# Two more early chunks flipped by TensorE, their masks and products on other engines, and a rebuilt order, in a gated attention with a feed-forward layer

## The chip, the cores and the metric

The kernel runs on one core of a Trainium2 chip. The metric is device microseconds of one execution. Before the change the median of three runs was 541.18 us (540.56 to 541.62).

## The reference

Two layers, in float32. The attention keeps, for each of 4 batches and 8 heads, a 48x48 state that decays by `alpha` at every one of 768 time steps; the feed-forward layer takes its output as 3072 rows of 384.

```python
for t in range(S):                                   # S = 768, q k v alpha: (4, 8, 768, 48)
    state = alpha[:, :, t, :, None] * state + np.einsum('bhd,bhe->bhde', k[:, :, t], v[:, :, t])
    y[:, :, t] = np.einsum('bhd,bhde->bhe', q[:, :, t], state)
x = y.transpose(0, 2, 1, 3).reshape(3072, 384)
h = x @ w_in                                         # (384, 2048), float64 in memory
g = np.where(h >= 1, h, np.where(h <= -1, 0.0, (h + 1) ** 2 / 4))
out = g @ w_out                                      # (2048, 384), float64 in memory
```

## The kernel before

**Chunks.** The sequence is cut into 24 chunks (0 to 23) of 128 time steps, six to a batch. For a chunk, `alpha`, `k` and `q` are wanted with the head dimension on partitions. Chunks below `EARLY` (7) are loaded as they lie, in rows of 48 numbers (192 bytes), and TensorE turns them into PSUM with three *flips* of four transposes each (L521). Later chunks are loaded twice over, by four transfers for each tensor in rows of 768 bytes, and VectorE turns them in SBUF (L534). VectorE then makes two running products of `alpha` (the scans L610 and L636), multiplies the backward one by `k` (L654), and the forward one is multiplied by `q` (L660): by VectorE out of PSUM for chunks 3 to 6 (`HELP` to `EARLY`); by GpSimd out of SBUF for the later ones and for chunks 0 to 2, whose flipped `q` ScalarE copies to SBUF first (L658). TensorE turns the product with `k`: this is the *keys' turn* of the chunk, K0 to K23 (L681). Score products follow (L696), state updates (L709), masks (L781 on VectorE; for half of them, in chunks below `HELP`, ScalarE copies and GpSimd multiplies by a mask, L754 and L760) and the chunk's output products (L835).

**Feed-forward.** Chunks go in groups of three. For each group and each f of 16 (128 columns of `w_in`), TensorE makes a *first product* of nine matmuls (L931); VectorE clips and takes a maximum (L975, L986), ScalarE squares and rounds (L960, L990), GpSimd makes the low part (L991); then come the nine matmuls of the *second product* (L1009). Groups 0 and 1 share each half of the weights: f 0 to 7 for both, then f 8 to 15 for both, then whole groups. First products are numbered here H1 to H128 and second ones F1 to F128, in TensorE's order. The weights come in eight units u0 to u7 of two f, as float64, and each half of a unit (`w_in`, `w_out`) is decoded into two float32 parts by ScalarE, VectorE (L370, L381) and GpSimd (L393, L405, each of which may go to VectorE instead). H7 and H8 are the first that need u3.

**Order.** Nothing is scheduled on the chip: each engine runs its instructions in the order in which the kernel wrote them. The class `Plan` sets that order: it walks through a list of operations with assumed durations and due times (`key`), and at each step takes the one that could start first, or, among those within `NEAR`, the one that is due first. An operation with a second engine is offered to both, there with its due time put off by `LATER`. Buffers count too: of the eight PSUM banks the attention may hold three (six for chunks below `ROOM`, by `FIRST`). Where TensorE would rest more than 0.45 us by the plan, before `WARMTH` of the plan's time, matmuls of zeros (L1080) are put in.

Due times follow from `FETCH` (weights), `DECODE`, `LOAD` (a chunk's loads), `MARGIN` and `AHEAD` (a chunk's own due time, L1088 to L1092).

Of the kernel before, what the change touches and what calls it, by code (L numbers as in the profile page):

```python
# [25 lines left out]
SLACK = 2.0**-15  # L26
GROUP = 3
SHARE = 2
EARLY = 7
MORE = 2  # L30
WARM = 20
LAG = 3.0
FETCH = 12.0
LOAD = 8.0
DECODE = 4.0
PREPARE = 2.5
MARGIN = 9.0
AHEAD = 12.0
FIRST = 6
ROOM = 4  # L40
LATER = 8.0
MERGE = 6
WARMTH = 60.0
HELP = 3
VHELP = 6
SPLIT = 0
CLIPS = 6.0
NEAR = 0.25


class Buf:
# [20 lines left out]
class Plan:  # L72
# [55 lines left out]
            ready.setdefault(way[0], []).append((o, i))  # L128

    def order(self):  # L130
        free = dict.fromkeys(("PE", "DVE", "ACT", "POOL", "SP"), 1.0)
        slots = {name: [(0.0, -i, None) for i in range(n)] for name, (n, share, _) in self.sizes.items() if share == name}
        live = {name: 0 for name in self.sizes}
        left = {}
# [92 lines left out]
def gated_attention_ffn(ctx: ExitStack, tc: tile.TileContext, q, k, v, alpha, w_in, w_out, out):  # L227
# [74 lines left out]
    with ExitStack() as main:  # L302
# [116 lines left out]
        def weights(u):  # L419
            fs = slice(u * NW * P, (u + 1) * NW * P)  # L420
            make = lambda shape, dt: Buf("wt", lambda: wts.tile(shape, dt, name="wt"))
            ti = make([P, KT, NW * P], w_in.dtype)
            to = make([P, NW, DM], w_out.dtype)
            key = need[u]
            pairs_of = w_in[0 : 2 * D * KT, fs].rearrange("(k r e) f -> r e k f", r=2, e=D)
            rest = w_in[2 * D * KT : DM, fs].rearrange("(r k e) f -> r e k f", r=2, k=KT)
            size = P * NW * DM * (8 if wide else 4)
            fetch = key - FETCH
            for r in range(2):
                p = 64 * r  # L430
                plan.op(
                    "SP",
                    Plan.ISSUE,
                    fetch,
                    lambda p=p, r=r: nc.sync.dma_start(out=ti()[p : p + D], in_=pairs_of[r]),
                    [],
                    [ti],
                    moved=size * 3 // 8,
                    beside=r > 0,
                )  # L440
                plan.op(
                    "SP",
                    Plan.ISSUE,
                    fetch,
                    lambda p=p, r=r: nc.sync.dma_start(out=ti()[p + D : p + 64], in_=rest[r]),
                    [],
                    [ti],
                    moved=size // 8,
                    beside=True,
                )  # L450
            plan.op(
                "SP",
                Plan.ISSUE,
                fetch,
                lambda: nc.sync.dma_start(out=to(), in_=w_out[fs, :].rearrange("(j p) m -> p j m", p=P)),
                [],
                [to],
                moved=size,
            )
            wi[u] = make([P, 2, KT, NW, P], F32R)  # L460
            wo[u] = make([P, 2, NW, DM], F32R)
            decode(u, "i", ti, wi[u], "p k f -> p (k f)", key - DECODE)
            decode(u, "o", to, wo[u], "p j m -> p (j m)", key - DECODE + LAG)


        C = CH // 32
# [10 lines left out]
        def load(x, j, key):  # L477
            b, t0 = j // PER, j % PER * CH
            t, rows = raws[x], {"a": alpha, "k": k, "q": q}[x][b, :, t0 : t0 + CH, :]
            if j < EARLY:  # L480
                if j < 2:
                    plan.op("POOL", 0.15, -99, lambda: nc.gpsimd.memset(whole(t, j)[:, :, D:], 1.0), [], [(x, j % 2)])
                plan.op(
                    "SP",
                    Plan.ISSUE,
                    key,
                    lambda: nc.sync.dma_start(out=whole(t, j)[:, :, 0:D], in_=rows.rearrange("h s d -> s h d")),
                    [],
                    [(x, j % 2)],
                    moved=P * DM * 4,  # L490
                )
                return
            if j == EARLY:
                plan.op(
                    "POOL", 0.15, key, lambda: nc.gpsimd.memset(t[:, :, W : W + 32], 1.0), [], [(x, 0), (x, 1)]
                )
            view = rows.rearrange("(g r) (a c) d -> r a g (c d)", r=2, c=C)
            for r in range(2):
                for half in range(2):
                    p0, o = 64 * r + 32 * half, 32 * (1 - half)  # L500
                    plan.op(
                        "SP",
                        Plan.ISSUE,
                        key,
                        lambda p0=p0, o=o, r=r: nc.sync.dma_start(out=t[p0 : p0 + 32, :, o : o + W], in_=view[r]),
                        [],
                        [(x, 0), (x, 1)],
                        moved=P * DM * 2,
                        beside=r + half > 0,
                    )  # L510

        def turned(x, j, key, to=()):

            t = raws[x]
            if j < EARLY:
# [8 lines left out]
                            identity=ident,  # L524
                        )

                flips[j] = plan.op("PE", 0.45, key, flip, [(x, j % 2)], [ps, *to], mode="full", after=[flips[j]] if j in flips else [])
                return ps, view
            o = buf("tp", "turn", [P, G * CH], 2)
            plan.op(  # L530
# [14 lines left out]
        def prepare(j, key):  # L545
# [107 lines left out]
            kt, kT = turned("k", j, key + 0.2)  # L653
            vec(0.66, lambda: nc.vector.tensor_tensor(out=flat(inv()), in0=flat(inv()), in1=kT(), op=ALU.mult), [inv, kt], [inv])  # L654
            qt, qT = turned("q", j, key + 0.2)
            if j < HELP:
                qs = buf("tp", "turn", [P, G * CH], 2)
                plan.op("ACT", 0.55, key + 0.2, lambda qT=qT: nc.scalar.copy(out=qs(), in_=qT()), [qt], [qs])  # L658
                qt, qT = qs, lambda: qs()
            mul = lambda e: e.tensor_tensor(out=flat(Q()), in0=flat(Q()), in1=qT(), op=ALU.mult)  # L660
            in_ps = HELP <= j < EARLY
            ways = [("DVE", 0.66, lambda: mul(nc.vector), not in_ps), ("POOL", 1.3, lambda: mul(nc.gpsimd), True)]
            (e, us, emit, port), other = ways if in_ps else reversed(ways)
            plan.op(e, us, key + 0.3, emit, [Q, qt, last], [Q], port=port, other=None if in_ps else other)
# [76 lines left out]
        def follow(j, key):  # L741
# [5 lines left out]
            for r, to in enumerate((Q, other)):  # L747
                for u in range(2):
                    if r and j < HELP:
# [7 lines left out]
                            beside=True,  # L757
                        )
                        if u:
                            cut = lambda e: e.tensor_tensor(  # L760
                                out=other()[0:HC].rearrange("p g (u t) -> p g u t", u=2),
                                in0=other()[0:HC].rearrange("p g (u t) -> p g u t", u=2),
                                in1=mask[0:HC, None, None, 0:HC].broadcast_to([HC, G, 2, HC]),
                                op=ALU.mult,
                            )
                            plan.op(
                                "POOL",
                                1.35,
                                key,
                                lambda: cut(nc.gpsimd),  # L770
                                [other],
                                [other],
                                port=True,
                                other=("DVE", 0.66, lambda: cut(nc.vector), True),
                            )
                        continue
                    plan.op(
# [309 lines left out]
        for j in range(NCH):  # L1087
            n = max(n for n in range(NG) if first[n] <= j)  # L1088
            since = begin[n - 1] if n > 0 else begin[n] - AHEAD
            due = since + (begin[n] - since) * (j - first[n] + 1) / groups[n] - MARGIN  # L1090
            prepare(j, due - PREPARE)
            attend(j, due)  # L1092
            done = j if j < MERGE or j == NCH - 1 else j - 1
# [173 lines left out]
```

## Time and profile before

| what | value |
|---|---|
| median of three runs | 541.18 us |
| the profiled execution: its time, its span | 542.22 us, 540.4 us |
| busy share of the span: TensorE, VectorE, ScalarE, GpSimd | 95%, 74%, 49%, 51% |
| matmuls of zeros (L1080) in the span | 149, 20.9 us |
| first and second products (L931, L1009) | 1152 matmuls each, 226.1 and 226.2 us |
| mean granted TensorE clock | 0.983 |

The time of an execution is 1.8 us more than its span, which runs from the first to the last instruction. TensorE's busy time counts overlapping matmuls only once, and a waiting TensorE that is given zeros is busy too; so the stretches and the gaps in the order of time say more than the share. "Idle before" is the time in which an engine stood still just ahead of an instruction, with the instruction that released it. DMA shares can pass 1 where transfers cross the edge of a stretch.

### The profile page before, as it was taken

The numbers are of one execution on the slowest core, as the hardware profiler recorded it, in microseconds if no ns is written. First come the engines' busy times: TensorE is split into PE (matmuls) and PEld (weight loads), VectorE is DVE, ScalarE is ACT, GpSimd is POOL, SyncE is SP. The second block draws the span as 40 slices with busy tenths as digits, with TensorE's granted clock in tenths as the row PEclk, the third lists the DMA queues.
The fourth block names the chain that finished last, engine by engine and source line by source line (L and its number), as shares of the span: only waits on it lengthen the run. The fifth ranks groups of instructions, "written<-read, shape, count | busy, mean of one in ns | idle before, by whom it ended". The sixth has DMA issues, their size and how long they took to land.

```text
span 540.4 us, 12713 instructions
## 1 busy us (share of the span) xinstructions
PE 516.0 (95%) x4923; PEld 494.9 (92%) x4923; DVE 399.3 (74%) x709; ACT 265.5 (49%) x490; POOL 276.0 (51%) x295
## 2 busy tenths in 40 slices
PE   8898979998589999999999999999999999999995
PEld 6787869987589999999999999999999999999995
DVE  4789889899988987967968887777787884334332
ACT  4668877676343444344354453444444544333332
POOL 7555888799955525425524543443543543233330
PEclk9989998999989999999999999999999999999999
DMA  9989699934044663334333444335324300101001
GB/s 178 196 173 225 146 210 197 268 74 118 7 111 134 146 154 90 87 79 122 86 77 96 102 105 106 100 61 140 96 45 116 90 16 3 22 1 44 2 0 49
DMA packets 109457, 55.05 MB, mean 102 GB/s; under 512 B 71536, under 2 KB 104272, under 8 KB 109392
## 3 DMA queue, kind: packets, MB, share of 16 engines
q1 hardware_dynamic: 109392, 54.19, 43.2%
q8 instruction: 40, 0.66, 0.5%
q14 instruction: 25, 0.20, 0.1%
HBM read 46.20 MB, written 5.90 MB: 96 GB/s over the span
## 4 chain that ended last, share of the span: by engine, by line
PE 79%; DVE 12%; issue 3%; ACT 2%; POOL 2%; DMA 1%; SPq 0%; DVEq 0%; ACTq 0%; POOLq 0%
PE ps L1009 33%; PE ps L931 33%; PE ps L835 5%; PE ps L709 2%; PE ps L681 2%; DVE w L381 2%; PE ps L1080 2%; PE ps L696 2%; DVE Q L610 2%; DVE inv L636 1%; DVE w L370 1%; DVE meet L649 1%; POOL wt L405 1%; DVE inv L654 1%; DVE gf L986 1%
## 5 line engine op out<-in xcount | busy, mean ns | idle before, releaser
L991 POOL TENSOR_TENSOR gh<-gf,gh 128x384 fp32r<-128x384 f32 x127 | 146.7, 1160 | 162.4 <-ACT gh L990 133.3
L1009 PE MATMUL ps<-wt,gh 128*128 128x384 f32 x1152 | 226.2, 341 | 2.1 <-POOL gh L991 2.1
L931 PE MATMUL ps<-ring,wt 128*128 128x384 f32 x1152 | 226.1, 343 | 1.9 <-POOL wt L405 1.8
L931 PEld LDWEIGHTS ps<-ring,wt 128*128 128x128 f32 x1152 | 205.3, 190 | 3.6 <-POOL wt L405 2.5
L1009 PEld LDWEIGHTS ps<-wt,gh 128*128 128x128 f32 x1152 | 202.9, 189 | 4.3 <-POOL gh L991 3.7
L960 ACT ACTIVATE gf<-gf,half_b 128x384 f32<-128x384 f32 x122 | 75.0, 616 | 114.3 <-DVE gf L975 90.9
L975 DVE TENSOR_SCALAR gf<-ps 128x384 f32<-128x384 f32 x122 | 67.0, 551 | 58.8 <-PE ps L931 50.1
L990 ACT CAST gh<-gf 128x384 fp32r<-128x384 f32 x128 | 65.7, 513 | 74.5 <-DVE gf L986 60.5
L986 DVE TENSOR_TENSOR gf<-gf,ps 128x384 f32<-128x384 f32 x128 | 70.0, 549 | 33.8 <-ACT gf L960 33.3
L728 ACT COPY both<-state 48x192 f32<-48x192 f32 x65 | 22.7, 350 | 45.4 <-POOL state L812 39.8
L405 POOL TENSOR_TENSOR wt<-w,wt 128x768 fp32r<-128x768 f32 x16 | 33.8, 2114 | 4.3 <-ACT wt L404 4.2
L393 POOL TENSOR_TENSOR w<-w,wt 128x768 int32<-128x768 int32 x14 | 27.4, 1960 | 10.1 <-DVE w L381 5.6
L660 POOL TENSOR_TENSOR Q<-Q,turn 128x512 f32<-128x512 f32 x20 | 25.8, 1292 | 7.2 <-DVE turn L534 5.9
L835 PE MATMUL ps<-other,both 128*64 128x64 f32 x372 | 27.9, 225 | 1.6 <-issue 1.5
L812 POOL TENSOR_TENSOR state<-state,last 128x192 f32<-128x192 f32 x20 | 11.3, 567 | 33.5 <-DVE state L738 33.4
L835 PE MATMUL ps<-Q,both 128*64 128x64 f32 x372 | 28.0, 226 | 0.1
L610 DVE TENSOR_TENSOR_SCAN Q<-turn,fwd 128x512 f32<-128x512 f32 x17 | 23.2, 1362 | 6.5 <-PE ps L835 6.4
L835 PEld LDWEIGHTS ps<-Q,both 128*64 128x64 f32 x372 | 24.0, 137 | 3.6 <-issue 1.5
L681 PE MATMUL ps<-ident,inv 128*128 128x128 f32 x96 | 15.2, 282 | 10.8 <-DVE inv L654 10.4
L781 DVE TENSOR_TENSOR Q<-ps,mask 64x256 f32<-64x256 f32 x48 | 20.3, 423 | 6.8 <-ACT other L746 5.3
L835 PEld LDWEIGHTS ps<-other,both 128*64 128x64 f32 x372 | 23.9, 137 | 1.1 <-issue 0.8
L681 PEld LDWEIGHTS ps<-ident,inv 128*128 128x128 f32 x96 | 11.7, 144 | 13.1 <-DVE inv L654 11.1
(89 smaller groups left out, 525.9 us busy)
## 6 DMA issues: line engine op xcount, KB each, us to landing
raw_a<-in_alpha SPq DMA_DIRECT2D x68, 96.0 KB, 2.4
raw_k<-in_k SPq DMA_DIRECT2D x68, 96.0 KB, 2.6
raw_q<-in_q SPq DMA_DIRECT2D x68, 96.0 KB, 2.3
wt<-in_moe_w_out SPq DMA_DIRECT2D x8, 768.0 KB, 9.8
vt<-in_v SPq DMA_DIRECT2D x24, 192.0 KB, 3.1
wt<-in_moe_w_in SPq DMA_DIRECT2D x16, 288.0 KB, 7.3
out<-ot SPq DMA_DIRECT2D x24, 192.0 KB, 2.4
both<-in_v SPq DMA_DIRECT2D x72, 48.0 KB, 2.4
```

The costliest lines, as they stand in the source:

```text
L393: add = lambda e: e.tensor_tensor(out=bits(), in0=bits(), in1=word(I32, 0), op=ALU.add)
L405: sub = lambda e: e.tensor_tensor(out=part(1), in0=data(), in1=part(0).bitcast(F32), op=ALU.subtract)
L610: lambda: nc.vector.tensor_tensor_scan(flat(Q()), aT(), flat(fwd), 0.0, ALU.mult, ALU.max),
L681: nc.tensor.transpose(out=kp()[:, g], in_=K()[:, g], identity=ident)
L835: nc.tensor.matmul(out=ps()[halves[r], to, halves[u]], lhsT=lhsT[:, u, r], rhs=x()[:, g, halves[u]], start=m + u == 0, stop=True, skip_gro ...
L931: nc.tensor.matmul(out=h(), lhsT=win(f, w)[:, kt], rhs=ring[:, at, kt, a, :], start=(m == 0), stop=(m == 3 * KT - 1),)
L960: lambda: nc.scalar.activation(out=gf(), in_=in_(), func=func, scale=scale, bias=bias),
L975: lambda: nc.vector.tensor_scalar(out=gf(), in0=h(), scalar1=-1.0, scalar2=1.0, op0=ALU.max, op1=ALU.min),
L986: lambda: nc.vector.tensor_tensor(out=gf(), in0=gf(), in1=h(), op=ALU.max),
L990: plan.op("ACT", 0.08 + 0.41 * w, key + 0.4, lambda: nc.scalar.copy(out=gh()[:, 0], in_=gf()), [gf], [gh])
L991: sub = lambda e: e.tensor_tensor(out=gh()[:, 1], in0=gf(), in1=gh()[:, 0].bitcast(F32), op=ALU.subtract)
L1009: nc.tensor.matmul(out=o_ps[seg][t](), lhsT=gh()[:, a, (t - c0) * CH : (t - c0 + 1) * CH], rhs=wout(f, w), start=(f == f0 and i == 0), sto ...
```

## The change

Chunks 7 and 8 now count as early ones (`EARLY` 9): their six flips (24 transposes) are TensorE's, into PSUM. No chunk copies its flipped `q` any more (`QHELP` 0), so in chunks 0 to 8 VectorE multiplies by `q` out of PSUM. Chunk 3 joins those whose second masks go over ScalarE and GpSimd (`HELP` 4), and GpSimd cuts with `affine_select` in place of a product with a mask. The other edits are numbers and rules of the plan: due times of loads, decodes and chunks (the first groups get their own margins, unit u0 its own fetch and decode times), `NEAR` 0, `LATER` 4, PSUM banks (`FIRST` 5, `ROOM` 2), zeros allowed up to 165 of the plan's time, and the pads of the early loads as operations of their own.

```diff
-EARLY = 7
+EARLY = 9
-LOAD = 8.0
-DECODE = 4.0
+LOAD = 6.0
+DECODE = 3.0
-MARGIN = 9.0
-AHEAD = 12.0
-FIRST = 6
-ROOM = 4
-LATER = 8.0
+MARGIN = 11.0
+MARGIN0 = 9.0
+MARGIN1 = 6.0
+FETCH0 = 18.0
+DECODE0 = 4.0
+AHEAD = 20.0
+FIRST = 5
+ROOM = 2
+LATER = 4.0
-WARMTH = 60.0
-HELP = 3
+WARMTH = 165.0
+QHELP = 0
+HELP = 4
-NEAR = 0.25
+NEAR = 0.0
...
-            fetch = key - FETCH
+            fetch = key - (FETCH if u else FETCH0)
+            ready = key - (DECODE if u else DECODE0)
...
-            if j < HELP:
+            if j < QHELP:
                 qs = buf("tp", "turn", [P, G * CH], 2)
...
-            in_ps = HELP <= j < EARLY
+            in_ps = QHELP <= j < EARLY
...
                             plan.op(
                                 "POOL",
-                                1.35,
+                                0.62,
                                 key,
-                                lambda: cut(nc.gpsimd),
+                                lambda: nc.gpsimd.affine_select(
+                                    out=other()[0:HC].rearrange("p g (u t) -> p g u t", u=2),
+                                    in_=other()[0:HC].rearrange("p g (u t) -> p g u t", u=2),
+                                    compare_op=ALU.is_ge,
+                                    fill=0.0,
+                                    base=0,
+                                    pattern=[[0, G], [0, 2], [1, HC]],
+                                    channel_multiplier=-1,
+                                ),
...
-            due = since + (begin[n] - since) * (j - first[n] + 1) / groups[n] - MARGIN
+            due = since + (begin[n] - since) * (j - first[n] + 1) / groups[n] - (MARGIN, MARGIN0, MARGIN1)[n + 1 if n < 2 else 0]
```

By the order, matmuls of zeros fall from 149 to 100, four of them behind K6; two subtractions of the decode (L405) move from GpSimd to VectorE and one of its additions (L393) moves back. Three places show how instructions move.

VectorE around the decode of unit u3, the half from `w_in` (before it is `wt_902` into `w_1146`, after `wt_886` into `w_994`; `inv_1167` and `inv_1133` are chunk 6, `inv_949` is chunk 5). Before:

```order
L636 SCALAR_TENSOR_TENSOR inv_1167<-ps_1124,bwd_79 128x511
L986 TENSOR_TENSOR gf_1119<-gf_1119,ps_1072 128x384
L370 TENSOR_SCALAR w_1146<-w_1146 128x768
L381 SCALAR_TENSOR_TENSOR w_1146<-wt_902,w_1146 128x768
L370 TENSOR_SCALAR w_1174<-w_1174 128x768
L649 TENSOR_TENSOR meet_82<-fwd_77,inv_1167 128x4
L986 TENSOR_TENSOR gf_1209<-gf_1209,ps_1133 128x384
L654 TENSOR_TENSOR inv_1167<-inv_1167,ps_1179 128x512
```

After:

```order
L660 TENSOR_TENSOR inv_949<-inv_949,ps_980 128x512
L666 TENSOR_TENSOR Q_924<-Q_924,ps_988 128x512
L386 SCALAR_TENSOR_TENSOR w_883<-wt_531,w_883 128x768
L375 TENSOR_SCALAR w_994<-w_994 128x768
L386 SCALAR_TENSOR_TENSOR w_994<-wt_886,w_994 128x768
L398 ISA w_994<-wt_886,w_994 128x1536
L788 TENSOR_TENSOR Q_924<-ps_1024,mask_65 64x4x64 x2
L788 TENSOR_TENSOR other_1056<-ps_1027,mask_65 64x4x64 x2
L744 TENSOR_TENSOR state_72<-state_72,ps_1024 128x192
L607 TENSOR_SCALAR fwd_77<-ps_1081 128x4
```

The decode stood between chunk 6's second scan and its product with `k`; it now stands ahead of the whole preparation of chunk 6, and its addition is VectorE's own (the row `ISA`). On TensorE, K6 has H6 and F4 ahead of it in both orders.

TensorE around the keys' turn of chunk 8, K8, the row with `inv`. Before:

```order
L1009 MATMUL ps<-wt,gh 128x384 x9
L931 MATMUL ps<-ring,wt 128x384 x9
L1009 MATMUL ps<-wt,gh 128x384 x9
L931 MATMUL ps<-ring,wt 128x384 x18
L681 MATMUL ps<-ident,inv 128x128 x4
L1009 MATMUL ps<-wt,gh 128x384 x9
L709 MATMUL ps<-vt,ks 64x48 x16
```

After:

```order
L527 MATMUL ps<-ident,raw_a 128x128 x4
L527 MATMUL ps<-ident,raw_k 128x128 x4
L1016 MATMUL ps<-wt,gh 128x384 x9
L938 MATMUL ps<-ring,wt 128x384 x9
L527 MATMUL ps<-ident,raw_q 128x128 x4
L1016 MATMUL ps<-wt,gh 128x384 x9
L938 MATMUL ps<-ring,wt 128x384 x9
L687 MATMUL ps<-ident,inv 128x128 x4
L1016 MATMUL ps<-wt,gh 128x384 x9
L938 MATMUL ps<-ring,wt 128x384 x9
```

K8 stood behind H24 and F20, now it stands behind H21 and F18, and the three flips of chunk 8 are in TensorE's own queue just ahead of it. K9 stood behind H28 and F26, now behind H27 and F24.

SP, which issues the loads, behind the loads of chunks 0 and 1 and the second `vt`. Before:

```order
L487 DMA raw_q<-in_q 128x8x48
L556 DMA vt<-in_v 128x8x48
L435 DMA wt<-in_moe_w_in 48x3x256
L445 DMA wt<-in_moe_w_in 16x3x256
```

After:

```order
L562 DMA vt<-in_v 128x8x48
L441 DMA wt<-in_moe_w_in 48x3x256
L451 DMA wt<-in_moe_w_in 16x3x256
L441 DMA wt<-in_moe_w_in 48x3x256
L451 DMA wt<-in_moe_w_in 16x3x256
L461 DMA wt<-in_moe_w_out 128x2x384
L493 DMA raw_a<-in_alpha 128x8x48
L493 DMA raw_k<-in_k 128x8x48
```

Unit u0 of the weights was issued behind the loads of chunks 2 and 3; it now goes ahead of both.

## Rows read from the trace of the kernel before

**Rows 1.** Three stretches, columns: stretch, its length, busy us per engine, clock, DMA.

```profile
0.00:76.00 76.00, 68.68 (x956) 58.69 (x956) 60.88 (x115) 51.65 (x97) 51.13 (x81) 0.98 0.90 188
76.00:170.50 94.50, 83.01 (x665) 79.60 (x666) 83.80 (x121) 55.84 (x95) 75.44 (x52) 0.93 0.56 133
170.50:527.00 356.50, 356.49 (x3263) 349.54 (x3262) 251.95 (x469) 154.30 (x292) 148.37 (x162) 1.00 0.32 77
```

**Rows 2.** TensorE in order of time: start, us, instruction, count, idle before.

```profile
75.99 0.66 PE L681 MATMUL ps<-ident,inv 128*128 128x128 f32 x4 [1.16 <-DVE inv L654]
...
77.21 0.62 PE L931 MATMUL ps<-ring,wt 128*128 128x384 f32 x2
79.62 5.49 PE L931 MATMUL ps<-ring,wt 128*128 128x384 f32 x16 [1.79 <-POOL wt L405]
85.04 0.88 PE L709 MATMUL ps<-vt,ks 64*64 64x48 f32 x32
...
150.06 1.12 PE L681 MATMUL ps<-ident,inv 128*128 128x128 f32 x4 [6.95 <-DVE inv L654]
...
153.92 0.68 PE L709 MATMUL ps<-vt,ks 64*64 64x48 f32 x32
...
167.27 3.34 PE L1009 MATMUL ps<-wt,gh 128*128 128x384 f32 x18
170.45 0.60 PE L681 MATMUL ps<-ident,inv 128*128 128x128 f32 x4
```

**Rows 3.** TensorE's waits from 76 to 170.5: total us, times, longest.

```profile
PE ps L1009 <- POOL gh L991: 1.9, 3, 1.2
```

**Rows 4.** VectorE by line, 76 to 170.5: busy us, mean ns, idle before.

```profile
L975 DVE TENSOR_SCALAR gf<-ps 128x384 f32<-128x384 f32 x21 | 11.4, 547 | 3.1 <-PE ps L931 3.1
L370 DVE TENSOR_SCALAR w<-w 128x768 int32<-128x768 int32 x9 | 8.1, 898 | 1.6 <-ACT w L354 1.6
L610 DVE TENSOR_TENSOR_SCAN Q<-turn,fwd 128x512 f32<-128x512 f32 x3 | 5.9, 1967 | 0.0
L636 DVE TENSOR_TENSOR_SCAN inv<-turn,bwd 128x511 f32<-128x511 f32 x3 | 5.4, 1797 | 0.0
L654 DVE TENSOR_TENSOR inv<-inv,turn 128x512 f32<-128x512 f32 x3 | 3.6, 1199 | 0.1
L534 DVE STREAM_TRANSPOSE turn<-raw_a 128x512 f32<-128x512 f32 x3 | 3.4, 1129 | 0.0
...
L393 DVE CUSTOM_DVE_ANT_0 w<-wt,w 128x1536 uint16<-128x1536 uint16 x1 | 1.8, 1778 | 0.0
```

**Rows 5.** VectorE by line, 0 to 76: the same lines reading PSUM.

```profile
L636 DVE TENSOR_TENSOR_SCAN inv<-ps,bwd 128x511 f32<-128x511 f32 x7 | 8.9, 1271 | 0.0
L610 DVE TENSOR_TENSOR_SCAN Q<-ps,fwd 128x512 f32<-128x512 f32 x7 | 8.6, 1224 | 0.2
...
L654 DVE TENSOR_TENSOR inv<-inv,ps 128x512 f32<-128x512 f32 x7 | 4.8, 686 | 0.6
...
L660 DVE TENSOR_TENSOR Q<-Q,ps 128x512 f32<-128x512 f32 x4 | 2.7, 677 | 0.0
```

**Rows 6.** TensorE from 18 to 32: flips of two chunks, matmuls of zeros.

```profile
19.37 0.66 PE L521 MATMUL ps<-ident,raw_a 128*128 128x128 f32 x4
...
20.74 1.36 PE L1080 MATMUL ps<-zeros 128*128 128x256 bf16 x11
...
27.66 1.11 PE L521 MATMUL ps<-ident,raw_k 128*128 128x128 f32 x4
...
29.42 2.42 PE L1080 MATMUL ps<-zeros 128*128 128x256 bf16 x14
```

**Rows 7.** GpSimd by line, whole span: the masks that it multiplies.

```profile
L760 POOL TENSOR_TENSOR other<-other,mask 64x512 f32<-64x512 f32 x3 | 3.8, 1264 | 0.9 <-ACT other L754 0.8
```

**Rows 8.** Two stretches of ten us, columns as in rows 1.

```profile
10.00:20.00 10.00, 9.11 (x220) 7.67 (x219) 6.59 (x16) 6.30 (x15) 5.80 (x12) 1.00 0.99 193
100.00:110.00 10.00, 10.00 (x61) 9.96 (x59) 9.67 (x14) 5.89 (x10) 6.40 (x7) 1.00 1.06 270
```

More of the change, by code (lines that the diff above doesn't have):

```diff
@@ L130, in order @@
     def order(self):
-        free = dict.fromkeys(("PE", "DVE", "ACT", "POOL", "SP"), 1.0)
+        free = {"PE": 1.0, "DVE": 1.0, "ACT": 1.0, "POOL": 5.0, "SP": 1.0}
         slots = {name: [(0.0, -i, None) for i in range(n)] for name, (n, share, _) in self.sizes.items() if share == name}
@@ L461, in weights @@
             wo[u] = make([P, 2, NW, DM], F32R)
-            decode(u, "i", ti, wi[u], "p k f -> p (k f)", key - DECODE)
-            decode(u, "o", to, wo[u], "p j m -> p (j m)", key - DECODE + LAG)
+            decode(u, "i", ti, wi[u], "p k f -> p (k f)", ready)
+            decode(u, "o", to, wo[u], "p j m -> p (j m)", ready + LAG)
         C = CH // 32
@@ L481, in load @@
                 if j < 2:
-                    plan.op("POOL", 0.15, -99, lambda: nc.gpsimd.memset(whole(t, j)[:, :, D:], 1.0), [], [(x, j % 2)])
+                    plan.op("POOL", 0.15, -99, lambda: nc.gpsimd.memset(whole(t, j)[:, :, D:], 1.0), [], [("pad", x, j)])
                 plan.op(
@@ L525, in flip @@
                         )
-                flips[j] = plan.op("PE", 0.45, key, flip, [(x, j % 2)], [ps, *to], mode="full", after=[flips[j]] if j in flips else [])
+                flips[j] = plan.op("PE", 0.45, key, flip, [(x, j % 2), ("pad", x, j % 2)], [ps, *to], mode="full", after=[flips[j]] if j in flips else [])
                 return ps, view
@@ L759, in follow @@
                         if u:
[L760 to L765, printed above, removed]
                             plan.op(
                                 "POOL",
-                                1.35,
+                                0.62,
                                 key,
-                                lambda: cut(nc.gpsimd),
+                                lambda: nc.gpsimd.affine_select(
[7 more added lines that the diff above has]
+                                ),
                                 [other],
@@ L773, in follow @@
                                 port=True,
-                                other=("DVE", 0.66, lambda: cut(nc.vector), True),
                             )
```

## The prediction, made before the changed kernel ran

> **What bounds the kernel now.** I read the page's strip of 40 slices first, then busy time by stretch, TensorE in order of time, its waits, and VectorE by line. From 170.5 us on TensorE never stops: 356.49 of 356.50 us busy at full clock [rows 1]. Whatever is lost there later would be new; what is lost now is lost before. So the question is how far TensorE's queue has come at some late point of the start. I take the keys' turns K6 (75.99 us) and K9 (170.45 us) as marks [rows 2].
>
> Between the two, by the order, lie H7 to H28 and F5 to F26: 44 products. Two of them, unhindered, take 3.18 us (167.27 to 170.45), so one takes 1.59 and all take 70.0. The stretch is 94.46 long. Its losses: H7 and H8 run from 77.21 to 85.04, 7.83 in place of 3.18, since H7 waits 1.79 us for the subtraction that ends the decode of u3 and the next 16 matmuls run 5.42 us, 0.34 each where 0.18 is usual: 4.65 lost. At K8 TensorE waits 6.95 for VectorE's product with `k`, and K8 with F21 then takes 3.86 where 1.59 and 0.60 are usual: 1.7 more [rows 2]. For GpSimd's low parts the second products wait 1.9 [rows 3]. That makes 15.2; 94.46 less 70.0 and 15.2 leaves 9.3 for the chunks' own matmuls. The granted clock is 0.93 there against 1.00 later [rows 1]; the two slow pieces are on its half level, 1.2 GHz, each behind a wait.
>
> VectorE is behind both big losses: it is busy 83.8 of the 94.5 us, and in the same stretch GpSimd 75.4 [rows 1]. Its operations on two SBUF tiles are long there: the scan L610 takes 1.97 and L654 1.20 [rows 4], against 1.22 and 0.69 where one operand comes out of PSUM [rows 5].
>
> **The change part by part.** *Up to K6.* VectorE makes three more products by `q` there (0.677 each, [rows 5]), and by the order one shift, one maximum, two masks and one ring row fewer, about as much. H6 and F4 stand ahead of K6 as before. VectorE was busy 60.9 of these 76 us [rows 1], so I leave K6 at 76, with -2 and +5 as bounds: unit u0 now loads ahead of chunk 2.
>
> *TensorE from K6 to K9.* It now holds H7 to H27 and F5 to F24: 41 products, 65.2 us. Added are six flips; three flips took from 19.37 to 20.74, so one takes 0.46 and six 2.7 [rows 6]. Four matmuls of zeros at 0.12 (eleven filled 1.36, [rows 6]) make 0.5. With the 9.3 of the chunks the work is 77.7. Then three products are owed before the old K9's state of work: 4.8. Together 82.5 against 94.46: if TensorE never waited, 12.0 us would be won.
>
> *VectorE from K6 to K9.* By the order: six transposes fewer, at 1.11 on the mean of the three tensors (first row [rows 4]): -6.7. Two pairs of scans go from SBUF to PSUM: 2 x (1.967 - 1.224 + 1.797 - 1.271) = -2.5. Two products with `k`: 2 x (1.199 - 0.686) = -1.0. One addition of the decode leaves: -1.8. Two products with `q` come: +1.35. Two subtractions of the decode come to VectorE, a form that it does not run before: 768 columns at L654's two prices for 512, times 1.5, is 1.03 or 1.80; I take the middle, two of them +2.9. The smaller rows that come and go nearly cancel. Sum -7.8: 83.8 becomes 76.0 [rows 1, 4, 5].
>
> So VectorE would be as long as TensorE, 76.0 against 77.7, if it never stood still. It stood still 10.7 us of this stretch; 3.1 of that were waits for late first products and 1.6 for buffers of the late decode [rows 4], which go with the stalls. I keep 6.0, so VectorE needs 82.0 and TensorE is held 4.3 us beyond its work, somewhere at K7, K8 or K9. Of the 12.0 then 7.7 stay. The bounds: no hold at all, 12.0; all 10.7 of standing still kept, VectorE 86.7, hold 9.0, won 3.0.
>
> *The u3 decode* is the reason why H7 need not wait: its VectorE part stands a whole chunk's preparation earlier in the order. What is late next is VectorE's queue.
>
> *Off the path.* Three copies of `q` leave ScalarE. GpSimd loses five products with `q`; the four cuts by `affine_select` replace three that take 1.26 [rows 7]. No row of this trace has that shape; between nothing and 1.26 each it costs GpSimd at most 5.1 in place of 3.8, in the first 50 us, where it works 51.1 of 76 [rows 1], and I take 1.26. Matmuls of zeros are no price where TensorE rests; there are fewer of them than before, so I give them no gain.
>
> *The loads.* Early chunks load half the bytes, in rows of 192 bytes. Between 10 and 20 us, where such rows prevail, the engines moved 193 GB/s at a share of 0.99; between 100 and 110, with weights and long rows, 270 at 1.06 [rows 8]. A chunk's 590 KB at 193 take 3.1 us, the late form's 1180 KB at 270 take 4.4: nothing is lost. The Trainium skill (DMA: Bandwidth & Descriptors, Specifications) says that transfers under 512 bytes fall short of line rate, which speaks against two more such chunks; the trace agrees on the rate and shows that the halved bytes outweigh it, so by either the sum keeps its value.
>
> *From K9 on* nothing changes but that VectorE hands a few output copies to ScalarE; TensorE is the bound.
>
> **The sum.** The profiled execution took 542.22 us (span 540.4, 1.8 around it): 542.22 - 7.7 = 534.5. The median of the runs lies 1.0 lower: 533.5.
>
> **The rivals.**
> *A: the wait stays whole.* VectorE stands still as before, and TensorE takes its 9.0 us in one wait behind which the clock falls again (1.7). Won 12.0 - 10.7 = 1.3: 539.9. For it: the assumed durations of the plan do not move with the contention that rows 4 show. Against: two of three scan pairs leave SBUF.
>
> *B: chunks 2 to 5 arrive late.* A unit of weights is 1.57 MB by its shape, 8.1 us at 193 GB/s [rows 8]; chunks 0 and 1 are as much again. So chunk 2 lands at 17 to 19 us, and its flips ran at 19.37 [rows 6]. If each of four chunks loses a little over 1 us, K6 comes 5 later: 538.5. Against: from chunk 3 on VectorE is later than the loads.
>
> *C: flips let the clock fall.* At 27.66 two flips took 1.76 us, 0.88 each against 0.46 [rows 6], after TensorE had stood still. Six at that price cost 2.5 more, and a product on the half level 1.5 more [rows 2]: with two such, 5.5, thus 539. Against: in the new order the flips lie between products. The Trainium skill (TensorE: Matmul & The Clock Gate, Part 4) states that the full clock does not come on for transposes. By it rival C would hold wherever flips follow a wait; the three flips from 19.37 ran at full speed, so the trace bears it out only in part.
>
> *D: slower, by TensorE's own queue.* A flip needs a free PSUM bank, and the attention has three: the flips of one chunk fill them, and VectorE frees them. Before, VectorE's transposes of chunks 7 and 8 kept TensorE out of this. Now a late VectorE halts it at Ta, Tk and Tq, with products queued behind. Price: one wait like that of K8 for each of the two chunks, 13.9 and 1.7 of clock, 15.6 against 12.0 to be won: 3.6 slower, 544.8. It is slower than before once these waits pass 12. Against: seven products (11 us) lie between chunk 7's burst and the first flip of chunk 8, enough for its masks.
>
> *E: better.* No hold, and K6 2 us earlier: 14.0 won, 527.
>
> **How the numbers follow.** Forecast 533.5, own range 529 to 538: 0.55. E 0.10, A 0.12, B 0.08, C 0.05, D 0.10. Range 526 to 541: it holds all but D and a few hundredths below. A measurement of this kernel tells 0.2% (1.1 us) from no change. Faster: 0.55 + 0.10 + 0.05 and most of A and B, 0.83; within 0.2%: the rest of A and B, 0.05; slower: D and mishaps like it, 0.12.
>
> **What would show it.** K6 at 74 to 81; H7 and H8 3.2 to 4 us with no wait for L410; VectorE busy about 76 us from K6 to K9; no single wait of TensorE for L660 above 4; K9 between 154 and 163 with three products fewer done; from there no gaps. Wrong would make it: scans of chunks 7 and 8 above 1.4 out of PSUM, K6 past 81, waits at L527 above 1 us each, or a gap behind 170.

## The result, and the profile after

The changed kernel takes 534.14 us (median of four runs, 533.86 to 534.57) against 541.40 for the kernel before beside it (540.56 to 541.78): a ratio of 0.9869, 95% interval 0.9852 to 0.9886. The forecast was 533.5. In the later rounds of e9 to e12 the same kernel took 535.63 (ratio 0.9895, 0.9872 to 0.9917), so its gain is 1.05 to 1.3%. The profiled execution took 533.86 us with a span of 532.1.

The three stretches of the trace of after, cut at K6 and K9, answer to [rows 1]; columns as there:

```profile
0.00:76.50 76.50, 62.00 (x899) 52.11 (x899) 63.53 (x116) 54.74 (x103) 45.89 (x73) 0.98 0.86 182
76.50:157.90 81.40, 77.72 (x669) 73.26 (x666) 69.53 (x115) 52.37 (x89) 63.88 (x50) 1.00 0.61 140
157.90:518.70 360.80, 360.78 (x3287) 354.20 (x3288) 244.17 (x468) 151.96 (x288) 144.84 (x173) 1.00 0.32 77
```

The first stretch is half a us longer than before. The second is 81.4 us in place of 94.5, with three products fewer in it (4.8 us), so 8.3 us were won here. The span shrank by as much (540.4 to 532.1): the half us by which K6 comes later is made good behind K9. The granted clock of the second stretch is 1.00 in place of 0.93. In the third, TensorE never stops, as before. VectorE is busy 69.5 us of the second stretch (83.8 before), and stands still 11.9.

TensorE in order of time, as in [rows 2]:

```profile
76.53 0.66 PE L687 MATMUL ps<-ident,inv 128*128 128x128 f32 x4
76.94 1.83 PE L938 MATMUL ps<-ring,wt 128*128 128x384 f32 x9
...
79.77 1.85 PE L938 MATMUL ps<-ring,wt 128*128 128x384 f32 x9
...
94.17 0.60 PE L527 MATMUL ps<-ident,raw_k 128*128 128x128 f32 x4
94.60 0.60 PE L527 MATMUL ps<-ident,raw_q 128*128 128x128 f32 x4
...
134.90 0.66 PE L687 MATMUL ps<-ident,inv 128*128 128x128 f32 x4 [0.17 <-DVE inv L660]
...
157.92 0.63 PE L687 MATMUL ps<-ident,inv 128*128 128x128 f32 x4 [0.21 <-DVE inv L660]
```

H7 and H8 (76.94 and 79.77) run at full speed with no wait for the decoding of u3. K8 (134.90) waits 0.17 where it waited 6.95. The flips of `k` and `q` of chunk 7 (94.17 and 94.60) are 0.43 apart and lie between products. What TensorE still waits for between K6 and K9 is at another place than forecast; the waits of that stretch (total us, times, longest) begin, all others being 0.5 or less:

```profile
PE ps L1016 <- POOL gh L998: 1.2, 1, 1.2
PE ps L1016 <- ACT gh L997: 1.1, 1, 1.1
```

Both waits for `gh` belong to one second product, F17; none is for VectorE's keys. VectorE by line, 76.5 to 157.9, answers to [rows 4]:

```profile
L375 DVE TENSOR_SCALAR w<-w 128x768 int32<-128x768 int32 x9 | 10.6, 1180 | 0.1
L386 DVE SCALAR_TENSOR_TENSOR w<-wt,w 128x768 int32<-128x768 int32 x9 | 10.1, 1121 | 0.1
L642 DVE TENSOR_TENSOR_SCAN inv<-ps,bwd 128x511 f32<-128x511 f32 x2 | 2.5, 1272 | 0.0
L616 DVE TENSOR_TENSOR_SCAN Q<-ps,fwd 128x512 f32<-128x512 f32 x2 | 2.4, 1223 | 0.1
L410 DVE TENSOR_TENSOR wt<-w,wt 128x768 fp32r<-128x768 f32 x2 | 2.2, 1124 | 0.2 <-ACT wt L409 0.2
...
L616 DVE TENSOR_TENSOR_SCAN Q<-turn,fwd 128x512 f32<-128x512 f32 x1 | 1.5, 1520 | 0.0
L642 DVE TENSOR_TENSOR_SCAN inv<-turn,bwd 128x511 f32<-128x511 f32 x1 | 1.3, 1274 | 0.0
```

The scans of chunks 7 and 8 out of PSUM take 1.22 and 1.27, as forecast. The one pair left in SBUF (chunk 9) takes 1.52 and 1.27; before, it took 1.22 and 1.28, and the means of 1.97 and 1.80 [rows 4] came from chunks 7 (1.86 and 1.27) and 8 (2.82 and 2.84). The "or" of the decode, L386, is a row that the prediction's sum left out: it takes 1.12 here and took 1.51 before, as L381 (10 times, 15.1 us).

What makes such rows long can be read from the two engines' rows of before side by side, here the forward scans of chunks 7, 8 and 9:

```profile
96.64 1.02 POOL L991 TENSOR_TENSOR gh<-gf,gh 128x384 fp32r<-128x384 f32 x1
96.88 1.86 DVE L610 TENSOR_TENSOR_SCAN Q<-turn,fwd 128x512 f32<-128x512 f32 x1
...
139.51 2.82 DVE L610 TENSOR_TENSOR_SCAN Q<-turn,fwd 128x512 f32<-128x512 f32 x1
...
164.56 1.22 DVE L610 TENSOR_TENSOR_SCAN Q<-turn,fwd 128x512 f32<-128x512 f32 x1
```

Chunk 7's scan began while GpSimd's L991 ran, and was done 1.08 us behind the end of that instruction (97.66). Chunk 8's began while an addition ran on GpSimd from 139.35 to 141.24, and was done 1.09 behind it. When chunk 9's began, GpSimd was idle. The "or" goes by the same pattern: where it begins while GpSimd is at work it ends 0.81 to 0.83 behind that instruction, and else takes 0.94 to 0.96. Seven of its ten rows of this stretch before began so, three of nine after.

A new stall stands ahead of K6. VectorE, GpSimd and TensorE of after behind K5 (61.83):

```profile
63.39 2.06 POOL L398 TENSOR_TENSOR w<-w,wt 128x768 int32<-128x768 int32 x1 [1.18 <-DVE w L386]
63.75 2.51 DVE L386 SCALAR_TENSOR_TENSOR w<-wt,w 128x768 int32<-128x768 int32 x1
...
66.06 0.66 PE L527 MATMUL ps<-ident,raw_a 128*128 128x128 f32 x4
66.40 1.54 DVE L398 CUSTOM_DVE_ANT_0 w<-wt,w 128x1536 uint16<-128x1536 uint16 x1
67.97 0.86 DVE L788 TENSOR_TENSOR Q<-ps,mask 64x256 f32<-64x256 f32 x2
...
69.80 1.09 PE L527 MATMUL ps<-ident,raw_k 128*128 128x128 f32 x4 [3.08 <-issue]
```

TensorE stands 3.08 us between the flips of `a` and `k` of chunk 6, though `raw_k` had landed. The banks were freed by the masks of chunk 5 (L788), whose last ended at 69.70, 0.10 ahead of the flip, and those stood behind 4 us of decoding for u3 (L386, L398). The flips and the 18 matmuls behind the rest then ran slow (1.09 us for four transposes, 4.12 us for 18 matmuls where 3.18 is usual). This is rival D's mechanism, one chunk earlier than the prediction put it.

### The profile page after: what moved, and what is told of

The parts are those of the page before. It is cut to its first block, busy times and chain, and to the rows that moved or that the text cites. A ratio compares the mean times of both kernels' runs of the same rounds, so it can differ in the third digit from the quotient of the medians.

```text
span 532.1 us, 12603 instructions
## 1 busy us (share of the span) xinstructions
PE 508.5 (96%) x4895; PEld 486.9 (92%) x4895; DVE 380.1 (71%) x703; ACT 262.8 (49%) x487; POOL 255.8 (48%) x296
## 4 chain that ended last, share of the span: by engine, by line
PE 81%; DVE 5%; issue 3%; SPq 3%; POOL 3%; ACT 2%; DMA 2%; DVEq 0%; ACTq 0%
PE ps L1016 35%; PE ps L938 34%; PE ps L842 4%; PE ps L715 2%; SPq L493 2%; PE ps L702 2%; PE ps L687 2%; POOL w L398 1%; PE ps L527 1%; DVE inv L642 1%; DMA vt<-in_v 1%; POOL wt L410 1%; DMA wt<-in_moe_w_in 1%; POOL gh L998 1%; DVE Q L616 1%
## 5 line engine op out<-in xcount | busy, mean ns | idle before, releaser
L998 POOL TENSOR_TENSOR gh<-gf,gh 128x384 fp32r<-128x384 f32 x127 | 136.6, 1076 | 175.4 <-ACT gh L997 146.9
L938 PEld LDWEIGHTS ps<-ring,wt 128*128 128x128 f32 x1152 | 203.0, 188 | 3.4 <-DVE ring L871 1.6
L997 ACT CAST gh<-gf 128x384 fp32r<-128x384 f32 x128 | 65.4, 512 | 69.5 <-DVE gf L993 57.2
L398 POOL TENSOR_TENSOR w<-w,wt 128x768 int32<-128x768 int32 x15 | 29.2, 1948 | 12.7 <-PE ps L1016 4.4
L690 ACT COPY ks<-ps 128x512 f32<-128x512 f32 x24 | 14.0, 585 | 27.8 <-PE ps L687 27.7
L410 POOL TENSOR_TENSOR wt<-w,wt 128x768 fp32r<-128x768 f32 x14 | 27.2, 1942 | 0.2
L788 DVE TENSOR_TENSOR Q<-ps,mask 64x256 f32<-64x256 f32 x48 | 20.3, 423 | 8.7 <-ACT other L752 7.1
L616 DVE TENSOR_TENSOR_SCAN Q<-turn,fwd 128x512 f32<-128x512 f32 x15 | 18.8, 1250 | 5.8 <-PE ps L842 5.8
L734 ACT COPY both<-state 48x192 f32<-48x192 f32 x52 | 18.2, 349 | 8.6 <-DVE state L744 4.8
L666 POOL TENSOR_TENSOR Q<-Q,turn 128x512 f32<-128x512 f32 x15 | 19.4, 1295 | 6.1 <-DVE turn L540 5.7
L386 DVE SCALAR_TENSOR_TENSOR w<-wt,w 128x768 int32<-128x768 int32 x16 | 19.9, 1241 | 0.2
```

The source lines that it names most:

```text
L398: add = lambda e: e.tensor_tensor(out=bits(), in0=bits(), in1=word(I32, 0), op=ALU.add)
L410: sub = lambda e: e.tensor_tensor(out=part(1), in0=data(), in1=part(0).bitcast(F32), op=ALU.subtract)
L616: lambda: nc.vector.tensor_tensor_scan(flat(Q()), aT(), flat(fwd), 0.0, ALU.mult, ALU.max),
L788: lambda r=r, u=u, to=to: nc.vector.tensor_tensor(out=to()[halves[1 - r], :, halves[u]], in0=ss(j, r)[halves[u]], in1=mask[halves[u], None ...
L938: nc.tensor.matmul(out=h(), lhsT=win(f, w)[:, kt], rhs=ring[:, at, kt, a, :], start=(m == 0), stop=(m == 3 * KT - 1),)
L997: plan.op("ACT", 0.08 + 0.41 * w, key + 0.4, lambda: nc.scalar.copy(out=gh()[:, 0], in_=gf()), [gf], [gh])
```

## The experiments

Three theories were to be told apart at first: the gain is VectorE's work, taken off by two more chunks on TensorE (V); it is the rebuilt order (O); it is the longer stretch of zeros (C). Each run has its own rounds with the kernel before, so ratios are compared.

**e1: seven chunks, all else as changed.** `-EARLY = 9` `+EARLY = 7`

> The changed kernel with seven chunks turned by TensorE instead of nine; the numbers of the order, the masks and the zeros stay as changed, and the order is planned anew for it. Theory V (what was won is VectorE's time between K6 and K9, by the six transposes and the scans beside them): VectorE is busy 78 to 84 us there again instead of 69.5, K6 to K9 lasts 88 us or more, and the time is 540 us (538 to 543). Theory O (the rebuilt order won it, by taking the decoding of unit 3 out of the way of TensorE's first products): K6 to K9 stays under 84 us and the time is 534 to 536 us.

Measured 544.53 us, ratio 1.0054 (1.0037 to 1.0070): slower than before. K6 to K9 (77.53 to 168.92):

```profile
77.53:168.92 91.39, 85.81 (x724) 80.56 (x721) 76.26 (x115) 52.67 (x92) 66.17 (x48) 0.96 0.57 137
```

The same 41 products take 10 us more than in after, 10.6 of TensorE's busy time there are matmuls of zeros, and K8 still waits 3.77 for the product with `k`. The stretch is as V expected (88 or more), VectorE's busy time a little under (76.3 for 78), the time 1.5 us over its range. Theory O is out as the whole cause.

**e2: nine chunks, the old order.** In the kernel before: `-EARLY = 7` `+EARLY = 9`

> The kernel before with nine chunks turned by TensorE instead of seven and nothing else changed (its own numbers of the order, its masks on GpSimd as a product, q of the first three chunks staged by ScalarE). Theory V: most of the gain is there alone, 535 to 537 us, with VectorE's busy time between K6 and K9 under 77 us. Theory O: 540 to 542 us, because the first product H7 still waits for the decoding of unit 3.

Measured 537.40, ratio 0.9918 (0.9897 to 0.9939). VectorE is busy 77.07 us from K6 to K9, with four products more in the stretch than in after, and its "or" takes 1.49 us as before. So the two chunks alone bring 0.8%, 0.4 us short of what V asked for at least. K8 does not wait here, and K7 to K8 lasts 34.15 us, where it lasted 40.42 before and lasts 33.53 in after:

```profile
110.04:144.19 34.15, 31.87 (x257) 30.42 (x258) 28.69 (x48) 18.79 (x32) 25.24 (x22) 0.95 0.24 62
```

H7 does not wait for u3 either, though VectorE starts on that decode at 70.18, as before (70.23); GpSimd's subtraction for it ended at 77.58 in place of 79.57. Theory O, which had H7 wait here, is out in this too.

**e3: the order alone.** In the kernel after: `EARLY = 7`, `QHELP = 3`, `HELP = 3`, the mask as a product again; what remains of the change are the numbers and rules of the order.

> The kernel before with the new numbers of the order and the longer stretch of zeros alone (seven chunks turned by TensorE, q of three chunks staged by ScalarE, the mask as a product on GpSimd or VectorE). Theory V: 540 to 543 us, no gain, since the wait of TensorE for the key tile at K8 (6.95 us before) is still there or as long in all. Theory O: 534 to 537 us.

Measured 539.51 (535.95 to 541.53), ratio 0.9967 (0.9950 to 0.9984): a small gain of its own, 0.3%, between the two expectations; its runs scatter most of all, and the profiled one is the fastest of the twelve. In its trace K8 waits only 0.36, but 61 matmuls of zeros (6.8 us) stand between K6 and K9, nearly all right behind K8: TensorE's rest has moved more than gone. By themselves the chunks (0.82%) and the numbers (0.33%) make 1.15%, and the whole change 1.05 to 1.31%. That these agree does not show that they add up: e1, with all but the two chunks, is 0.5% slower than before, so beside the rest of the change the two chunks are worth 1.6 to 1.9 points. e1 against e3 (0.9 points slower) shows that the parts left over (q out of PSUM in chunks 0 to 2, a fourth chunk helped, `affine_select`), or the order that the plan makes with them, cost something with seven chunks. Whether nine chunks with the new numbers and the old help would be faster still was not run.

**e4: u3's decode behind the masks of chunk 5.** The two VectorE steps of the first half move in the finished order:

```diff
-for o in plan.order():
+line, mark = plan.order(), marks[5]
+shift = [o for o in line if o in late[3, "i"] and line.index(o) < line.index(mark)]
+line = [o for o in line if o not in shift]
+at = line.index(mark) + 1
+for o in line[:at] + shift + line[at:]:
     o.emit()
```

> The changed kernel with one swap on VectorE alone: the two steps of the decoding of unit 3's first half, which stand ahead of the masks of chunk 5 (2.51 and 1.54 us in the trace of after), stand behind them. Theory M (these two steps held the masks, and so the PSUM banks that TensorE's flip of k of chunk 6 needed): that flip starts at 66 to 68 us instead of 69.8, K6 comes at 72 to 74 us instead of 76.5, and the time is 530 to 532 us. Rival G (VectorE and not TensorE's start limits the stretch up to K9, so an earlier K6 is given back there): K6 earlier, but K9 at 157 to 158 us and 533.5 to 534.5 us. Rival W (H7 then waits for the decoding that was moved): a wait of 2 us or more at H7, and 533 to 535 us.

Measured 536.99, ratio 0.9919 (0.9904 to 0.9935): no gain; theory M in this form fell, and so did the times of G and W. Counted from K5, the masks began 4.40 us on in place of 6.14: of the 4 us of decode moved away 1.7 came through, since they now waited 2.52 us for the products with `v` (L716), which need ScalarE's copy of the turned keys. So the decode in after had in part filled a wait. And the flip of `q` came 3.85 us behind that of `k`, since it needs the bank that the addition to the state frees, and that now stood behind the decode. K6 came 16.99 us after K5, where it came 14.70 in after.

**e5 and e10: six transposes put back.** Into after, with nothing reading them, ahead of the first scan and of the two products in chunks 7 and 8; e10 is the same with strided views:

```diff
+def spend():
+    if j in (7, 8):
+        nc.vector.transpose(out=pools["tp"].tile([P, G * CH], F32, name="turn", bufs=2), in_=flat(fwd))
...
-vec(0.66, lambda: nc.vector.tensor_tensor(out=flat(inv()), in0=flat(inv()), in1=kT(), op=ALU.mult), [inv, kt], [inv])
+vec(0.66, lambda: (spend(), nc.vector.tensor_tensor(out=flat(inv()), in0=flat(inv()), in1=kT(), op=ALU.mult)), [inv, kt], [inv])
...
```

> The changed kernel with six more transposes of 128x512 on VectorE, three each in chunks 7 and 8 at the places where the kernel before had them (ahead of the first scan, of the product with k and of the product with q); they turn a constant and nothing reads what they write, and the order of everything else is that of after. Theory V (VectorE's own work sets the pace from K6 to K9): six of 1.1 us come back whole, VectorE's busy time there rises from 69.5 to 76 us, and the time is 539 to 541 us. Theory S (VectorE stands still 11.9 us of that stretch in after and TensorE is busy 77.7 of 81.4, so there is room): 0 to 3 us of it show, 534 to 537 us.

> As e5, but with the six transposes in the strides of the kernel before (every fourth element written), so that one takes 1.1 us instead of the 0.69 us that it took there: 6.6 us of VectorE put back between K6 and K9. Theory V (VectorE's own time is the limit there): 5 us or more over e9. Theory S (it has 11.9 us to spare, and what the six cost is the delay of a chunk's own chain, as the 1.0 us from K6 to K9 in e5): 1 to 3 us over e9.

e5 measured 537.10, ratio 0.9924 (0.9899 to 0.9950), but its transposes were only 0.69 us long, so e10 was made. e10 measured 537.78, ratio 0.9916 (0.9892 to 0.9940), against 535.63 for after in the same rounds. VectorE's transposes in e10 (in e5 they are 4.2 us, 694 ns each):

```profile
L607 DVE STREAM_TRANSPOSE turn<-fwd 128x512 f32<-128x512 f32 x6 | 6.7, 1111 | 0.0
```

6.7 us of work cost 2.15 us of time, by medians whose intervals overlap: theory S. The traces say the same: K6 to K9 lasts 83.28 us in e10, 81.39 in after and 81.69 in e9, and VectorE, busy 72.29 us of it in e10 (68.33 in e9), still stands still 11. In after VectorE's own busy time is no longer the limit of these chunks. Put back, the transposes cost some 2 of the 7.3 us won; how the rest divides between the scans, the products with `k` and the "or" was not run.

**e6: zeros up to 60 us of the plan.** `-WARMTH = 165.0` `+WARMTH = 60.0`

> The changed kernel with zeros multiplied up to 60 us of the plan as before, instead of 165. By the plan this takes away four matmuls of zeros in all (behind H8, at 81.5 us). Theory N (the longer stretch does nothing here): 533.5 to 535 us, and the clock from K6 to K9 stays at 0.98 or more. Theory C (the zeros hold the clock): the flip of a of chunk 7 at half clock and 536 us or more.

Measured 535.35, ratio 0.9896 (0.9871 to 0.9921), as after in e9 (0.9895). The flip of `a` of chunk 7, with no zeros ahead, took 0.60 us. Theory N by the time: this part of the change does nothing that shows, and with nine chunks on TensorE the plan finds one rest to fill. N's other sign failed: the granted clock from K6 to K9 was 0.96 in this trace, where N asked for 0.98.

**e7: masks and state first, keys copied first.** As e4, but with `mark = grown[5, 0]` (the addition to the state), and ScalarE's copy of chunk 5's turned keys right behind the turn.

> The changed kernel with two steps moved at chunk 5. On VectorE both steps of the decoding of unit 3's first half (2.51 and 1.54 us) go behind the masks and behind the addition to the state, which is what the flip of q of chunk 6 waits for. On ScalarE the copy of the turned keys of chunk 5 goes right behind the step that follows the turn, since the masks wait for the products with v that read it. Theory M2 (the masks and the addition held the flips of k and q of chunk 6, in that order): from the flip of a to that of k is under 2 us (3.74 in after), the flip of q follows within 1 us, K6 comes 1.5 to 3 us earlier counted from K5 (14.7 us in after), and the time is 531 to 533 us. Rival G (what is won ahead of K6 is given back up to K9): 533.5 to 535 us. Rival W (H7 waits for the decoding that was moved): 535 to 537 us.

Measured 535.55, ratio 0.9893 (0.9873 to 0.9913): no gain. The flips came as M2 said (2.01 us from `a` to `k`, 0.47 to `q`), but the next piece was late, in TensorE's order of e7:

```profile
66.10 0.66 PE L528 MATMUL ps<-ident,raw_a 128*128 128x128 f32 x4
68.11 0.63 PE L528 MATMUL ps<-ident,raw_k 128*128 128x128 f32 x4 [1.36 <-issue]
68.58 1.01 PE L528 MATMUL ps<-ident,raw_q 128*128 128x128 f32 x4
...
70.98 5.25 PE L1019 MATMUL ps<-wt,gh 128*128 128x384 f32 x17 [1.07 <-POOL wt L411]
```

GpSimd's low part of u1 was not there, and 17 matmuls took 5.25 us, 0.31 each where 0.18 is usual. K6 came 14.76 us after K5, as in after, so the gain was given back ahead of K6 and not, as rival G has it, behind. H7 did not wait (rival W).

**e8: the mask as a product.** GpSimd's `affine_select` back to `tensor_tensor` with the mask, same order.

> The changed kernel with the mask of chunks 0 to 3 on GpSimd as a product with a tile of ones and zeros instead of affine_select, planned at the same cost so that the order is the same. Theory A (GpSimd's mask lies on the way of the first chunks' outputs): a product of 1.2 to 1.4 us against 0.66 makes K3 to K6 0.5 to 2.5 us later, 534.5 to 536.5 us. Theory B (it is hidden): 533.5 to 534.5 us.

Measured 536.38, ratio 0.9915 (0.9888 to 0.9942). A product takes 1264 ns, `affine_select` 662. The time points to theory A, but its interval covers after's 0.9895, and its K5 (62.74) lies among those of the runs that keep `affine_select` (61.39 in e6 to 63.29 in e4); not settled.

**e9: after again**, to hold the next three against.

> The changed kernel as it is, on the chip and in the rounds of the next three, so that they have something to be held against: 533.5 to 536 us.

Measured 535.63 (534.87 to 537.40). Its trace has the same 3.08 us rest, and a worse slow piece behind it: 5.37 us for the 18 matmuls, K6 15.93 after K5 (14.70 in the first trace).

**e11: zeros in the rest at chunk 6.** Into a bank that already holds a sum, with `start=False`, since no bank is free there:

```diff
+def add_zeros(n):
+    for _ in range(n):
+        nc.tensor.matmul(out=o_ps[segs[0]][0]()[:, 0:256], lhsT=zeros, rhs=nothing, start=False, stop=False)
...
 for o in plan.order():
     o.emit()
+    if o is turns["a", 6]:
+        add_zeros(24)
```

> The changed kernel with 24 matmuls of zeros behind the flip of a of chunk 6, where TensorE stood 3.08 us; they add nothing to a bank that holds a sum already, since no bank is free there. Theory C (the clock that fell in that rest made the flips and the second products behind it slow): the two flips take 0.6 us instead of 1.1, the 18 matmuls behind them 3.2 instead of 4.1, K6 comes 13 to 14 us after K5 instead of 14.7, and the time is 0.7 to 1.7 us under e9. Rival D (VectorE's products of chunk 6 end no earlier, so K6 waits for them): the same as e9 within 0.5 us.

Measured 534.64 (533.53 to 534.96), ratio 0.9862 (0.9841 to 0.9884), 1.0 us under e9 by medians; the intervals overlap. TensorE of e11, then of e9:

```profile
67.71 2.78 PE L1096 MATMUL ps<-zeros 128*128 128x256 bf16 x24
70.95 0.63 PE L528 MATMUL ps<-ident,raw_k 128*128 128x128 f32 x4 [0.46 <-issue]
71.42 0.60 PE L528 MATMUL ps<-ident,raw_q 128*128 128x128 f32 x4
71.78 3.43 PE L1020 MATMUL ps<-wt,gh 128*128 128x384 f32 x18
76.22 0.66 PE L689 MATMUL ps<-ident,inv 128*128 128x128 f32 x4
83.77 0.63 PE L528 MATMUL ps<-ident,raw_a 128*128 128x128 f32 x4 [1.99 <-issue]
```

```profile
70.74 1.06 PE L527 MATMUL ps<-ident,raw_q 128*128 128x128 f32 x4
71.45 5.37 PE L1016 MATMUL ps<-wt,gh 128*128 128x384 f32 x18
77.83 0.66 PE L687 MATMUL ps<-ident,inv 128*128 128x128 f32 x4
84.64 0.63 PE L527 MATMUL ps<-ident,raw_a 128*128 128x128 f32 x4 [1.25 <-issue]
```

Theory C holds for the piece: K6 comes 13.23 us after K5 instead of 15.93 (14.70 in the first trace). Then 0.7 of it goes at the next flip, which waits 1.99 in place of 1.25, and 1.6 in the 18 matmuls behind that (4.94 us, 3.37 in e9). The stretch from K5 to the flip of `a` of chunk 7 shows why, VectorE third, in e11 and then in the first trace of after:

```profile
62.99:83.77 20.78, 17.77 (x238) 15.59 (x238) 19.96 (x33) 18.19 (x31) 15.07 (x12) 1.00 0.37 83
61.83:82.61 20.78, 16.61 (x214) 14.73 (x214) 19.77 (x33) 18.10 (x31) 15.03 (x12) 0.92 0.44 95
```

VectorE is busy 19.96 of 20.78 us there (96%), 25.4 of 32.0 from K7 to K8. The stretch is just as long in after, with the rest and the slow pieces in it, and K9 comes 96.1 us after K5 in both; so the zeros won only against the slower trace of e9 (97.6). The flip starts 0.10 behind the end of VectorE's copy out of PSUM that follows the masks (L742 at 82.51 in after, L746 at 83.67 in e11). Around chunk 6 VectorE is still the limit.

**e12: e7 with zeros** (ten behind each of the flips of `a` and `q`).

> The kernel of e7 with ten matmuls of zeros behind the flip of a and ten behind the flip of q of chunk 6. Theory C: the 17 matmuls that took 5.25 us in e7 take 3.0 to 3.3, K6 comes 12.5 to 13.5 us after K5 (14.76 in e7), and the time is 1 to 2.2 us under e9. Rival D (K6 then waits for VectorE's product with k, which ended at 75.8 us in e7, 13.3 us after K5): K6 13.4 us after K5 or later, and 0 to 1 us under e9.

Measured 536.90, ratio 0.9905 (0.9879 to 0.9932). K6 came 13.54 us after K5, theory C's piece (17 matmuls in 3.23 us) and rival D's bound at once; but K6 to K7 then lasted 28.9 us (25.5 in e9), with waits of 1.49 for GpSimd's L411 and 1.80 for ScalarE's output copy. Won ahead of K6, lost behind it: the time is 1.3 us over e9 by medians, where both theories had it under.

## Why the prediction was right, and where not

**The time** is 0.6 us off, and so is K9 (157.92; the working gives 76 + 82 = 158). The mechanism that it named, VectorE's queue ahead of K8, is shown: H7's wait for u3 and K8's wait for the keys are gone, with their slow pieces behind them; the two chunks alone (e2) take K7 to K8 nearly to where after has it, and without them (e1) K8 waits again. Why H7 no longer waits is open: the prediction put it down to the earlier place of u3's decode on VectorE, and e2 has no such wait with the decode in its old place.

**"VectorE busy 76.0, standing still 6.0"** is the step that was wrong in its two terms (69.5 and 11.9); that their sum came out (82.0 against 81.4) is luck. The busy time fell by 14.3 us [rows 1], not 7.8. The transposes gave the -6.7 forecast, the scans -3.6 for -2.5, the product with `k` -1.5 for -1.0 (0.68 to 0.69 each now), the products with `q` +0.7 for +1.35, since chunk 6's moved ahead of K6. The scans and the product with `k` were priced at the mean of three chunks, but those of chunks 7 and 8 were the long ones: chunk 8's two scans took 5.66 us, chunk 9's 2.50, because GpSimd was at work when they began. The term left out is the "or" of the decode: 15.1 (L381) became 10.1, of which one instruction fewer is 1.5 and a shorter mean 3.5; the shift (8.1 us in [rows 4], now L375) took 2.5 back. The mean of the "or" from 62 to 170 us is 1.48 before, 1.46 in e2, 1.35 in e3, 1.26 in e1 and 1.21 in after: it follows the new order, not the two chunks.

**"TensorE is held 4.3, at K7, K8 or K9"**: held 3.7 (81.4 less its 77.7 of work), but mostly at F17 for GpSimd and ScalarE. e10 shows why it is not VectorE: of 6.7 us put back on it 2.15 came through. Before, it was the limit, from K7 to K8 above all, where before and after read:

```profile
109.64:150.06 40.42, 30.71 (x255) 28.94 (x253) 37.58 (x47) 24.25 (x41) 37.57 (x23) 0.96 0.27 66
```

```profile
101.37:134.90 33.53, 30.82 (x257) 28.51 (x255) 27.16 (x42) 22.59 (x37) 26.95 (x21) 1.00 0.65 160
```

VectorE worked 37.58 of 40.42 us, and GpSimd as long; now it works 27.16 of 33.53. A mean over K6 to K9 hid that K8's wait came from this third alone.

**K6 at 76** held (76.53), but by luck in part: TensorE lost 3.08 us and about 1 to 2 of clock at chunk 6, which the prediction had not seen, and VectorE was busy 63.5 us there where it had left the 60.9 [rows 1] as they were. What made up for it was not looked into. Rival D looked for such a stall in chunks 7 and 8 only, where no flip waited over 0.6 us in this trace (1.25 in e9).

**The smaller terms.** `affine_select` took 0.66 us, inside 0 to 1.26 but far from the value taken. The two subtractions cost 2.2 for 2.9. The loads lost nothing (K2 at 25.91 against 25.61). Zeros got no gain in the sum and have none (e6). From K9 on TensorE has no gap.

**The rivals.** A and D as priced (waits of 7 at K8) did not come; B is out by K2 and K6; C is out behind products, where four transposes take 0.60 us, and true behind a rest, at chunk 6. The three flips from 19.37, which the prediction held against C, followed matmuls without a wait, so they did not test it. E fell by the 3.7 us of hold and the stall ahead of K6.

## What to carry to other kernels

Sum busy time between the waits, not over a long stretch: one chunk's preparation at 93% on VectorE made the whole wait, while the two others stood at 85 and 86% (17.34 of 20.39 us and 28.85 of 33.65). Price the rows that go one by one, not at the mean of their group: a row that waits for a neighbour is long by what was left of the neighbour's instruction, so a new order alone makes it longer or shorter, as it did the "or". And a gain ahead of a full engine is given back there (e11), so ask which engine is full right behind the place that is mended.

## What the runs showed of the hardware

- VectorE and GpSimd stop each other in SBUF. One "or" took 0.94 us at 62.30 in after and 2.51 at 63.75; there GpSimd's addition ran until 65.45, and 0.81 us later the "or" was done, as if it had stood until then. The custom addition took 1.54 in after and 2.44 in e4, and ended 0.81 behind GpSimd's instruction both times (67.13 and 72.07). Scans in SBUF ended 1.08 or 1.09 behind (96.88, 139.51 and 143.13 before, 152.58 in after) and took 1.22 where GpSimd was idle at their start; out of PSUM a scan took 1.22 beside a GpSimd addition that was running (83.80 in after). It goes the other way too: GpSimd's low part, 1.02 us alone, took 1.75 at 65.38 and ended 0.87 behind that "or". The Trainium skill (SBUF — State Buffer, Who interferes with whom) says that the two share a port pair under an exclusive lock, and that the loser blocks; for these rows the trace agrees.
- After a rest of 3.08 us TensorE's 18 matmuls took 4.12 us in one execution and 5.37 in another, against 3.43 with zeros in the rest; the granted clock from K5 to the flip of `a` of chunk 7 was 0.92, 0.85 and 1.00. The Trainium skill (TensorE: Matmul & The Clock Gate, Part 4) says that the full clock does not come on for transposes. The flips behind the rest (1.09 and 1.06 us) agree, but so did the products behind them run slow, and the flips between products took 0.60 at full speed; no run here tells transposes from other work in this.
- A transpose of 128x512 on VectorE took 0.69 us between contiguous tiles (e5) and 1.11 when it wrote every fourth element (e10).
